# Sink attention's row sums: the step that inverts them moved ahead in VectorE's order, and their transposition behind the probabilities' in TensorE's

## The chip, the core and the metric

The kernel runs on one core of a Trainium2 chip. A core has five instruction streams that run side by side and meet only through semaphores: TensorE (PE in the profile; its weight loads have a row of their own, PEld), VectorE (DVE), ScalarE (ACT), GpSimd (POOL) and the DMA-issuing SyncE (SP). Each stream runs its instructions strictly in the order in which they were written; a waiting instruction holds back all that stand behind it. The metric is the device time of one execution in microseconds (us), the median of several runs.

## What is computed

Three layers, chained: attention with sink tokens and a sliding window over 2 batches, 8 heads, 768 positions of 64 columns; a convolutional MLP; and a mixture of four causal attention experts. The change touches the first alone:

```python
scores = scale * np.matmul(q, k.transpose(0, 1, 3, 2))
keep = is_sink | in_window            # n_sink = 4, window = 128
scores = np.where(keep, scores, -1000000000.0)
scores = scores - np.max(scores, axis=-1, keepdims=True)
a = np.exp(scores)
a = a / (np.sum(a, axis=-1, keepdims=True) + 1e-09)
return np.matmul(a, v).astype(np.float32)
...
x = _moe_ref(x=x, **moe_kwargs)       # relu(x @ w_in), 3-tap convolution, gate, @ w_out
return _moe2_ref(x=x, **moe2_kwargs)  # four experts: causal attention, top 2
```

The MLP's weights come as 64-bit floats and are converted on the chip, each into a high and a low part.

## The kernel before

**Tiles and steps.** A batch's attention goes over 6 tiles of 128 queries (qt) and, in each, over 4 pairs of heads (pr): 24 steps. A step i has stages that are spread over later steps. `a1_S` (lines 449 to 492) makes the scores: TensorE multiplies into two banks of PSUM, one for each head (L484 in the first batch, L471 in the second), VectorE adds the mask and takes the row's maximum (L486, twice), and ScalarE takes the exponential and the row's sum (L489, twice; the sums go into `su`, 8 columns for the 8 heads of a tile). `a1_T` transposes the probabilities on TensorE (L545) and copies them out of PSUM (L501, on ScalarE, tile `PT`). `a1_V` multiplies them with v (L587).

**The row sums.** They are not divided out of the probabilities; the tile's output is scaled afterwards. When the fourth pair of a tile is done, `a1_r` adds 1e-9 to the 128 x 8 sums and inverts them on VectorE (L496, L497). `a1_rT` transposes them to 8 x 128 on TensorE (L514), copies that out of PSUM (L501 on ScalarE in the first batch, L503 on VectorE in the second; tile `rT`) and sends it to memory (L518, tile `rD`). `a1_rB` reads it back, spread over 128 partitions (L525, tile `R`), and `x_norm` multiplies (L529). This happens 12 times, 6 in each batch.

**What else runs there.** In both batches' attention the MLP's weights are converted beside the steps, one weight tile of 128 x 512 after another: L339 on ScalarE, then L343, L346 and L349 on VectorE (tiles `raw` and `f64u`), then the high part on a varying engine (L507 or L509) and the low part on VectorE (L413). From the second batch's seventh step on, the MLP of the first batch runs interleaved (L753 to L797).

**What sets the order.** Nothing is scheduled at run time. `run_phases` puts each stage of each step at a time (the stage's start, plus its lag, plus the step's number times the rate), and within one time sorts by the stage's place in a list of names, the string ORD1. There `a0` is the first batch's attention, `a1` the second's, `m` the MLP; `.r`, `.rT`, `.S`, `.T` are the stages above, and `a0.misc`, `a1.misc`, `.more` and `m.misc` issue loads and the conversion's pieces. The lags are not touched: `r` runs one step after the tile's fourth pair, `rT` two steps after, in both batches.

```python
    for t in sorted(at):
        for _, _, i, fn in sorted(at[t], key=lambda c: c[:3]):
            fn(i)
...
    def a1_r(self, b, qt):
        r = self.a1s[(b, qt)]
        self.nc.vector.tensor_scalar(r, r, EPS, None, op0=ALU.add)
        self.nc.vector.reciprocal(r, r)
```

Of the kernel before, what the change touches and what calls it, by code (L numbers as in the profile page):

```python
# [74 lines left out]
LAGM = (1, 2, 3)  # L75
A2_N = 2
EVT = 'aaadadada'
ORD1 = 'm.rest a0.more a1.T a0.gather m.more m.H a1.gather a1.rB m.gate a0.xl m.Y a1.S a1.V a1.sV a1.xl a1.r a0.S a1.halo a0.sL late a0.V a0.rB a0.sV a0.xm a1.more a1.sT a0.halo a0.rT a1.xm a1.misc a1.xh a0.sT a0.T a0.misc a1.sL a0.r a1.rT m.conv m.misc a0.xh'
ORD2 = 'q1 c0.V c0.T c0.S0 c1.V c1.T c1.S0 out c0.W c0.S1 qlo c0.norm c1.W in c1.S1 q0'
ENG_G = 'pp'  # L80
WHI = 'aadaddapdpaaddda'
# [7 lines left out]
class Kernel:  # L89
# [1027 lines left out]
    def program(self, general):  # L1117
# [5 lines left out]
        with ExitStack() as ctx:  # L1123
# [89 lines left out]
            else:  # L1213
                a0, a1 = first
                src = {"a0": a0, "a1": a1, "m": m, "late": late}
                ph = self.order(ORD1, src)
            qlo = (t, t1 + 60, [(0, lambda i: self.run_qlater())], 1)
# [71 lines left out]
```

## Time and profile before

| what | value |
|---|---|
| median of 3 runs | 371.52 us (371.45 to 371.52) |
| the profiled execution: its time | 371.99 us |
| its span (first to last instruction) | 370.1 us |
| PE, DVE, ACT, POOL busy, share of the span | 97%, 74%, 71%, 32% |
| mean granted TensorE clock | 0.996 |

The first batch's attention fills the stretch from about 6 to 57 us, the second's from there to about 170 us with the MLP interleaved from 57 us on; the MLP's second half and the experts follow. The page's share for PE, 97%, counts matmuls whose ends are modelled, so it does not say by itself that TensorE is what every stage waits for. In the chain of waits TensorE's work stands almost alone from about 97 to 141 us and from about 155 us to the end; from about 57 to 95 us it is VectorE's, with turns through ScalarE; ahead of that TensorE's and VectorE's pieces alternate. What a stage waits for is read from three views: the chain of waits (which work, followed back from the end, was released last), the timeline with the idle time ahead of each instruction and who ended it, and the busy time in stretches.

### The profile page before, as it was taken

The numbers are of one execution on the slowest core, as the hardware profiler recorded it, in microseconds if no ns is written. First come the engines' busy times: TensorE is split into PE (matmuls) and PEld (weight loads), VectorE is DVE, ScalarE is ACT, GpSimd is POOL, SyncE is SP. The second block draws the span as 40 slices with busy tenths as digits, with TensorE's granted clock in tenths as the row PEclk, the third lists the DMA queues.
The fourth block names the chain that finished last, engine by engine and source line by source line (L and its number), as shares of the span: only waits on it lengthen the run. The fifth ranks groups of instructions, "written<-read, shape, count | busy, mean of one in ns | idle before, by whom it ended". The sixth has DMA issues, their size and how long they took to land.

```text
span 370.1 us, 8877 instructions
## 1 busy us (share of the span) xinstructions
PE 359.7 (97%) x3166; PEld 331.7 (90%) x3166; DVE 273.1 (74%) x850; ACT 261.2 (71%) x746; POOL 118.8 (32%) x230
## 2 busy tenths in 40 slices
PE   8999999899999999999999999999999999999994
PEld 5687877899899999999999999999999899978983
DVE  5689899999887997878756766238668688578731
ACT  4999998766886766546746766249878687849841
POOL 7014120444432342844421322500034144406310
PEclk9999999999999999999999999999999999999998
DMA  7943865353342311000211010000000010101112
GB/s 178 362 140 126 241 220 173 116 186 129 103 128 69 105 30 31 6 25 25 63 44 45 1 58 3 0 2 0 2 3 1 17 42 22 40 0 58 58 51 75
DMA packets 20404, 27.53 MB, mean 74 GB/s; under 512 B 2080, under 2 KB 12928, under 8 KB 20352
## 3 DMA queue, kind: packets, MB, share of 16 engines
q1 hardware_dynamic: 19120, 26.22, 22.2%
q10 hardware_dynamic: 1232, 0.66, 0.9%
q8 instruction: 27, 0.44, 0.5%
q14 instruction: 25, 0.20, 0.2%
HBM read 23.68 MB, written 3.19 MB: 73 GB/s over the span
## 4 chain that ended last, share of the span: by engine, by line
PE 77%; DVE 12%; ACT 5%; issue 2%; POOL 2%; DMA 1%; SPq 0%; ACTq 0%; DVEq 0%
PE psB L797 15%; PE psB L753 14%; PE psB L947 9%; PE psB L1061 5%; PE psB L1037 5%; PE psB L875 5%; PE psB L1085 4%; PE psB L587 4%; PE psB L484 4%; PE psB L545 3%; DVE P L486 3%; PE psB L1008 3%; PE psB L1007 3%; PE psB L471 2%; ACT P L489 2%
## 5 line engine op out<-in xcount | busy, mean ns | idle before, releaser
L797 PE MATMUL psB<-g,wouthf 128*128 128x256 f32 x384 | 70.5, 281 | 0.2 <-POOL g L782 0.2
L797 PEld LDWEIGHTS psB<-g,wouthf 128*128 128x128 f32 x384 | 58.9, 188 | 0.6 <-POOL g L782 0.4
L753 PE MATMUL psB<-xh,winhf 128*128 128x258 f32 x192 | 56.5, 294 | 0.0
L1025 POOL TENSOR_SCALAR P<-P,r 128x256 f32<-128x256 f32 (+5 forms) x48 | 30.3, 644 | 79.4 <-DVE r L1023 32.6
L753 PE MATMUL psB<-xh,winlf 128*128 128x258 f32 x192 | 54.3, 283 | 0.0
L753 PE MATMUL psB<-xl,winhf 128*128 128x258 f32 x192 | 54.2, 282 | 0.0
L797 PE MATMUL psB<-g,woutlf 128*128 128x256 f32 x192 | 53.8, 280 | 0.0
L489 ACT ACTIVATE P<-P,nm 128x260 f32<-128x260 f32 (+2 forms) x96 | 46.5, 486 | 10.1 <-DVE nm L486 9.9
L782 POOL TENSOR_TENSOR g<-ht,g 128x256 fp32r<-128x256 f32 x48 | 33.2, 691 | 52.4 <-ACT g L776 46.9
L1014 ACT ACTIVATE P<-P,nm 128x256 f32<-128x256 f32 (+5 forms) x48 | 32.1, 669 | 13.5 <-DVE nm L1013 7.8
L769 ACT ACTIVATE ht<-ht 128x256 f32<-128x256 f32 x48 | 20.1, 418 | 28.3 <-DVE ht L767 28.2
L774 DVE SCALAR_TENSOR_TENSOR ht<-ht 128x256 f32<-128x256 f32 x48 | 24.2, 505 | 18.8 <-ACT ht L769 18.8
L753 PEld LDWEIGHTS psB<-xh,winhf 128*128 128x128 f32 x192 | 36.4, 189 | 0.3 <-ACT ht L756 0.2
L753 PEld LDWEIGHTS psB<-xl,winhf 128*128 128x128 f32 x192 | 36.5, 190 | 0.0
L753 PEld LDWEIGHTS psB<-xh,winlf 128*128 128x128 f32 x192 | 36.2, 189 | 0.0
L797 PEld LDWEIGHTS psB<-g,woutlf 128*128 128x128 f32 x192 | 36.2, 189 | 0.0
L1010 DVE CUSTOM_DVE_ANT_0 P<-psB,causal 128x384 f32<-128x384 f32 (+3 forms) x64 | 30.3, 503 | 5.7 <-PE psB L1008 5.2
L760 POOL TENSOR_SCALAR ht<-ht,cw 128x256 f32<-128x256 f32 x24 | 15.1, 627 | 59.8 <-ACT ht L756 52.3
L767 DVE SCALAR_TENSOR_TENSOR ht<-ht,cw 128x256 f32<-128x256 f32 x48 | 28.3, 589 | 1.7
L545 PE MATMUL psB<-ident,P 128*128 128x128 f32 x176 | 29.0, 281 | 0.2
L947 PE MATMUL psB<-yh,wqh 128*128 128x256 f32 x96 | 27.2, 283 | 0.0
L947 PE MATMUL psB<-yl,wqh 128*128 128x256 f32 x96 | 27.0, 281 | 0.0
(172 smaller groups left out, 961.3 us busy)
## 6 DMA issues: line engine op xcount, KB each, us to landing
raw<-in_w_in_dram SPq DMA_DIRECT2D x8, 512.0 KB, 4.1
raw<-in_w_out_dram SPq DMA_DIRECT2D x8, 512.0 KB, 3.3
v<-in_v_dram SPq DMA_DIRECT2D x12, 256.0 KB, 4.4
R<-rD SPq DMA_DIRECT2D x24, 128.0 KB, 2.9
out_dram<-ot SPq DMA_DIRECT2D x11, 256.0 KB, 2.0
k<-in_k_dram SPq DMA_DIRECT2D x7, 260.0 KB, 3.6
raw<-in_wqkv_dram SPq DMA_DIRECT2D x8, 193.0 KB, 3.0
q<-in_q_dram SPq DMA_DIRECT2D x6, 256.0 KB, 4.5
```

What stands on the lines that cost most here:

```text
L489: nc.scalar.activation(Pt[:, j, :N], Pt[:, j, :N], AF.Exp, bias=nmx[:, j : j + 1], scale=-1.0, accum_out=sums[:, j : j + 1])
L545: nc.tensor.transpose(ps[:, j, c, :], Pt[:, j, c0 : c0 + P], self.ident)
L753: nc.tensor.matmul(ps[:, :XW], w[:, f, kc, :], x[:, kc, :], start=(i == 0), stop=(i == len(ops) - 1))
L767: nc.vector.scalar_tensor_tensor(t1, h[:, 2 : 2 + CH], self.cw[:, 2 * NF + f : 2 * NF + f + 1], t1, op0=ALU.mult, op1=ALU.add)
L769: nc.scalar.activation(t1, t1, AF.Tanh)
L774: nc.vector.scalar_tensor_tensor(t1, t1, 1.0, h[:, 1 : 1 + CH], op0=ALU.add, op1=ALU.mult)
L782: eng.tensor_tensor(g[:, 1], t1, g[:, 0].bitcast(F32), op=ALU.subtract)
L797: nc.tensor.matmul(self.m1y[d // 2][:, d % 2, :], w[:, f, d, :], g[:, k], start=(first and i == 0 and d % 2 == 0), stop=(last and i == 2), ...
L947: nc.tensor.matmul(ps, w[:, kc, c0 : c0 + P], y[:, kc, :], start=(i == 0), stop=(i == len(ops) - 1))
L1010: nc.vector.tensor_tensor_reduce(out=Pt[:, lo:hi], in0=ps[:, : hi - lo], in1=mask, scale=-1.0, scalar=BIG, op0=ALU.add, op1=ALU.min, accum ...
L1014: nc.scalar.activation(Pt[:, :N], Pt[:, :N], AF.Exp, bias=nm[:, 0:1], scale=-1.0, accum_out=sums[:, j : j + 1])
L1025: nc.gpsimd.tensor_scalar(Ps[j][:, :N], Ps[j][:, :N], r[:, j : j + 1], 1.0, op0=ALU.mult, op1=ALU.mult)
```

## The change

One string is changed, the order of the stages' names. Three names move: `a1.r` from behind `a1.xl` to ahead of `a1.S`; `a0.r` from behind `a1.sL` (that is, behind the conversion's pieces) to directly behind `a0.S`; and `a0.rT` from ahead of `a1.xm` to directly behind `a0.T`.

```diff
-ORD1 = '... m.Y a1.S a1.V a1.sV a1.xl a1.r a0.S ... a0.halo a0.rT a1.xm a1.misc a1.xh a0.sT a0.T a0.misc a1.sL a0.r a1.rT ...'
+ORD1 = '... m.Y a1.r a1.S a1.V a1.sV a1.xl a0.S a0.r ... a0.halo a1.xm a1.misc a1.xh a0.sT a0.T a0.rT a0.misc a1.sL a1.rT ...'
```

No instruction is added or taken away. On VectorE ten of the twelve pairs L496, L497 stand elsewhere (the second batch's last two stand where they stood); on TensorE five of twelve L514; on ScalarE five copies of `rT`; on SyncE one L518.

First batch, VectorE, the step after the fourth query tile's last pair (`su_470` is that tile's sums; the number behind a name is a buffer's):

```order
 L486 ISA nm_591 128x1
-L349 SCALAR_TENSOR_TENSOR f64u_500<-raw_376,f64u_500 128x512
 L496 TENSOR_SCALAR su_470<-su_470 128x8
 L497 RECIPROCAL su_470<-su_470 128x8
+L349 SCALAR_TENSOR_TENSOR f64u_502<-raw_378,f64u_502 128x512
 L486 ISA P_635,nm_636<-psB_633,m0x 128x260
```

The two small instructions stood behind the conversion's L349 and now stand ahead of it. The first batch's other five places read alike; at the first of them three conversions of 128 x 24 stand in L349's place.

First batch, TensorE, one step later, the same tile:

```order
 L484 MATMUL psB_633<-k_128,q_121 128x260
 L484 MATMUL psB_634<-k_128,q_121 128x260
-L514 MATMUL psB_643<-ident,su_470 8x128
-L545 MATMUL psB_649<-ident,P_590 128x128 x4
+L545 MATMUL psB_643<-ident,P_590 128x128 x4
+L514 MATMUL psB_650<-ident,su_470 8x128
 L484 MATMUL psB_662<-k_128,q_121 128x260
```

The transposition of the sums changed places with the four transpositions of the step's probabilities; the copies on ScalarE follow suit. So at five places; at the sixth, the batch's last tile, there is no such swap.

Second batch, VectorE, the step after the first query tile's last pair, before:

```order
L617 TENSOR_TENSOR xl_955<-R_883,xh_954 128x4x128
L486 ISA P_991,nm_992<-psB_989,m_69 128x256
L486 ISA nm_992 128x1
L486 ISA P_991,nm_992<-psB_990,m_69 128x256
L486 ISA nm_992 128x1
L496 TENSOR_SCALAR su_867<-su_867 128x8
L497 RECIPROCAL su_867<-su_867 128x8
L349 SCALAR_TENSOR_TENSOR f64u_894<-raw_762,f64u_894 128x512
```

The same place, after:

```order
L617 TENSOR_TENSOR xl_955<-R_885,xh_954 128x4x128
L496 TENSOR_SCALAR su_867<-su_867 128x8
L497 RECIPROCAL su_867<-su_867 128x8
L486 ISA P_993,nm_994<-psB_991,m_69 128x256
L486 ISA nm_994 128x1
L486 ISA P_993,nm_994<-psB_992,m_69 128x256
L486 ISA nm_994 128x1
L349 SCALAR_TENSOR_TENSOR f64u_896<-raw_764,f64u_896 128x512
```

Here the two small instructions went ahead of the step's masked scores, L486. Three more places of the second batch read alike, and TensorE's order is the same as before in this batch.

## Rows read from the trace of the kernel before

**Rows 1.** Busy time in one stretch: length, then busy us (instructions) of PE, PEld, DVE, ACT, POOL, clock, DMA:

```profile
100.00:141.00 41.00, 41.00 (x393) 38.44 (x395) 35.79 (x94) 29.41 (x87) 14.90 (x36) 1.00 0.25 79
```

**Rows 2.** Timeline of TensorE's weight loads: start, duration, engine, line, tile, [idle ahead <-releaser]:

```profile
12.69 0.08 PEld L514 LDWEIGHTS psB<-ident,su 128*8 128x8 f32 x1 [0.65 <-DVE su L497]
17.30 0.30 PEld L484 LDWEIGHTS psB<-k,q 128*128 128x128 f32 x2 [0.31 <-DMA q<-in_q_dram]
...
36.74 0.08 PEld L514 LDWEIGHTS psB<-ident,su 128*8 128x8 f32 x1 [0.64 <-ACT P L489]
...
52.75 0.08 PEld L514 LDWEIGHTS psB<-ident,su 128*8 128x8 f32 x1 [0.28 <-DVE su L497]
...
58.86 0.08 PEld L514 LDWEIGHTS psB<-ident,su 128*8 128x8 f32 x1 [0.49 <-DVE su L497]
...
71.86 0.08 PEld L514 LDWEIGHTS psB<-ident,su 128*8 128x8 f32 x1 [1.14 <-ACT P L489]
...
74.86 0.30 PEld L797 LDWEIGHTS psB<-g,wouthf 128*128 128x128 f32 x2 [0.24 <-ACT PT L501]
```

**Rows 3.** Timeline of all engines, 35 to 38 us:

```profile
35.62 0.69 DVE L349 SCALAR_TENSOR_TENSOR f64u<-raw,f64u 128x512 int32<-128x512 int32 x1
35.90 0.50 ACT L489 ACTIVATE P<-P,nm 128x260 f32<-128x260 f32 x1
36.23 0.16 DVE L496 TENSOR_SCALAR su<-su 128x8 f32<-128x8 f32 x1
36.42 0.20 DVE L497 RECIPROCAL su<-su 128x8 f32<-128x8 f32 x1
36.87 0.42 PEld L545 LDWEIGHTS psB<-ident,P 128*128 128x128 f32 x4
37.26 0.74 PEld L484 LDWEIGHTS psB<-k,q 128*128 128x128 f32 x4
```

**Rows 4.** Timeline of all engines, 44 to 45 us:

```profile
44.49 0.59 ACT L501 COPY PT<-psB 128x512 f32<-128x512 f32 x1 [0.35 <-PE psB L545]
44.98 0.43 DVE L486 CUSTOM_DVE_ANT_0 P<-psB,m1x 128x260 f32<-128x260 f32 x1 [0.72 <-PE psB L484]
```

**Rows 5.** Timeline of DVE and POOL, 26 to 30 us, and at 51.7 us:

```profile
26.37 0.69 DVE L349 SCALAR_TENSOR_TENSOR f64u<-raw,f64u 128x512 int32<-128x512 int32 x1
27.16 1.27 POOL L295 TENSOR_TENSOR vsr<-vs,vsr 32x512 fp32r<-32x512 f32 x1 [2.73 <-issue]
29.09 1.28 POOL L295 TENSOR_TENSOR vsr<-vs,vsr 32x512 fp32r<-32x512 f32 x1
29.18 1.46 DVE L343 TENSOR_SCALAR f64u<-f64u 128x512 int32<-128x512 int32 x1 [0.49 <-ACT f64u L339]
...
51.70 0.69 DVE L349 SCALAR_TENSOR_TENSOR f64u<-raw,f64u 128x512 int32<-128x512 int32 x1
51.75 0.68 POOL L626 CAST xl<-xl 128x4 fp32r<-128x4 f32 x1
```

**Rows 6.** Timeline of DVE and ACT, 57 to 60 us:

```profile
57.20 0.19 ACT L489 ACTIVATION_READ_ACCUMULATOR P<-P,nm 128x1 f32 x1
57.71 0.42 DVE L486 CUSTOM_DVE_ANT_0 P<-psB,m 128x256 f32<-128x256 f32 x1
58.17 0.51 ACT L489 ACTIVATE P<-P,nm 128x256 f32<-128x256 f32 x1 [0.53 <-DVE nm L486]
58.40 0.17 DVE L496 TENSOR_SCALAR su<-su 128x8 f32<-128x8 f32 x1
58.72 0.64 DVE L349 SCALAR_TENSOR_TENSOR f64u<-raw,f64u 128x512 int32<-128x512 int32 x1
59.96 0.43 DVE L343 TENSOR_SCALAR f64u<-f64u 128x512 int32<-128x512 int32 x1 [0.60 <-ACT f64u L339]
```

**Rows 7.** Timeline of ACT, 73 and 92 us:

```profile
73.27 0.42 ACT L769 ACTIVATE ht<-ht 128x256 f32<-128x256 f32 x1 [1.07 <-DVE ht L767]
...
92.35 1.07 ACT L810 COPY y<-psB 128x512 f32<-128x512 f32 x2
```

More of the change, by code (lines that the diff above doesn't have):

```diff
@@ L77 @@
 EVT = 'aaadadada'
-ORD1 = 'm.rest a0.more a1.T a0.gather m.more m.H a1.gather a1.rB m.gate a0.xl m.Y a1.S a1.V a1.sV a1.xl a1.r a0.S a1.halo a0.sL late a0.V a0.rB a0.sV a0.xm a1.more a1.sT a0.halo a0.rT a1.xm a1.misc a1.xh a0.sT a0.T a0.misc a1.sL a0.r a1.rT m.conv m.misc a0.xh'
+ORD1 = 'm.rest a0.more a1.T a0.gather m.more m.H a1.gather a1.rB m.gate a0.xl m.Y a1.r a1.S a1.V a1.sV a1.xl a0.S a0.r a1.halo a0.sL late a0.V a0.rB a0.sV a0.xm a1.more a1.sT a0.halo a1.xm a1.misc a1.xh a0.sT a0.T a0.rT a0.misc a1.sL a1.rT m.conv m.misc a0.xh'
 ORD2 = 'q1 c0.V c0.T c0.S0 c1.V c1.T c1.S0 out c0.W c0.S1 qlo c0.norm c1.W in c1.S1 q0'
```

## The prediction, on record before the changed kernel ran

> **What bounds the kernel now.** I read the chain of waits first. From about 97 to 141 us and from 155 us to the end it runs on TensorE almost alone; in the stretch from 100 to 141 us TensorE is busy 41.00 of 41.00 us [rows 1]. There, an instruction of VectorE that comes 0.3 us sooner or later moves nothing. The change can only tell where TensorE really waits, or where another engine sets the pace: in the first batch's attention, up to 57 us, where TensorE, ScalarE and VectorE are all nearly full, and from 57 to 95 us, where the chain runs on VectorE with turns through ScalarE.
>
> The second view is the idle time ahead of each weight load, for the twelve L514. Seven have none to speak of (a gap of 0.17 us stands ahead of most groups). Five waited: 0.65, 0.64, 0.28, 0.49 and 1.14 us [rows 2], 3.20 us in all. This is the most that the change can give back directly. The question for each is whether that wait is what the next stage needed.
>
> **What each part costs or gives.** Nothing is added, so every term is a shift. The price of a moved pair L496, L497 is the time from the start of L496 to the start of what follows it: 58.72 - 58.40 = 0.32 us [rows 6]; at 36.2 us it reads the same way, 0.16 and 0.20 us long with their overlap [rows 3].
>
> First batch, the wait of 0.64 us at 36.74. L514 stood ahead of the probabilities' transpositions and waited for L497, which stood behind L349; those transpositions started at 36.87, the next scores' weights at 37.26 [rows 3]. In the new order the transpositions wait for their exponentials alone: the second one begins at 35.90 and takes 0.50 us, so they end at about 36.40 [rows 3], and TensorE starts some 0.1 us later, at 36.5. Then come L514 (0.08 to 0.13 us) and the scores, at about 37.05 in place of 37.26. The gain is about 0.2 us. It is not eaten up on the way: at 44.49 ScalarE waited 0.35 us for TensorE and at 44.98 VectorE waited 0.72 us for it [rows 4], so both follow a TensorE that is earlier by up to 0.35 us, and from there VectorE runs without a gap into the second batch.
>
> First batch, the wait of 0.65 us at 12.69. The transpositions' own exponentials end only about 0.1 us before, so little is won, and at 17.30 TensorE waits 0.31 us for a load of q [rows 2], which no part of the change issues sooner. Term: 0. The wait of 0.28 us at 52.75: TensorE gets L514 earlier, but the scores behind it go to VectorE, whose L349 and scores need the same sum of time in either order. Term: 0. The other three places of this batch had no wait. Term: 0. The copy of `rT` now stands behind that of `PT`, so `rD` leaves about half a microsecond later; the first one is queued behind loads anyway, and SyncE's order otherwise changes at one place only. I put this at 0: between the issue of `R` and its use several microseconds of steps lie.
>
> First batch, third place, at 26.37. There was no wait of TensorE here, but a neighbour. L349 moves back by 0.32 us and then ends at 26.37 + 0.32 + 0.69 = 27.38, less an overlap of up to 0.08, that is 27.30 to 27.38. GpSimd's L295 wants to start at 27.16 [rows 5]. The row at 51.75 shows what happens then: a cast of 4 columns by GpSimd, begun 0.05 us after an L349, took 0.68 us and ended with it (52.43 against 52.39). So L295 would lose 0.14 to 0.22 us, and with it the chain behind it on GpSimd, up to the second L295 at 29.09, which would start at 29.23 to 29.31. In the trace that second L295 started 0.09 us before VectorE's L343 (29.18), and L343 took 1.46 us [rows 5] where the same instruction takes 0.43 us [rows 6]. L343 would now come first, by 0.05 to 0.13 us, and end about 1.0 us sooner. What is then late next is TensorE, which runs without a wait from there to the 0.64 us at 36.74: scores, masks and exponentials follow it, and of the 1.0 us there remains what makes the exponentials at 35.90 earlier, about 0.3 us. The transpositions then start behind the scores at about 36.3, the next scores at 36.8 in place of 37.26: the gain of this batch becomes 0.48 us in place of 0.2 us.
>
> The Trainium skill, "SBUF — State Buffer", section "Who interferes with whom", says that an instruction of VectorE with two inputs in SBUF and one of GpSimd that reads SBUF exclude each other, and that whichever is issued first keeps the ports for its whole length. It names this case's pairs (L349 with L295, and L343 as a two-port instruction), and the 0.68 and 1.46 us agree with it. By that rule alone the swap at 29.18 is certain, and the first batch gives 0.48 us.
>
> By the rows the swap hangs on 0.05 to 0.13 us between two engines that are not in step, and I give it 60%.
>
> Second batch, first place, at 57.71. Here the chain of waits goes through what the change delays. VectorE masks the scores (57.71), ScalarE, idle for 0.53 us, starts the exponentials at 58.17, then converts (L339), and VectorE, idle for 0.60 us, goes on with L343 at 59.96 [rows 6]. The pair now stands ahead of the masks, so masks, exponentials, L339 and L343 all come 0.32 us later. The sums that the pair needs are read out at 57.39 [rows 6], so no wait comes on top. The 0.49 us that TensorE no longer waits at 58.86 [rows 2] buys nothing, since L343 does not depend on it. Term: +0.32 us, and VectorE carries it to about 95 us, where TensorE waits for it in turn.
>
> Second batch, second place, the wait of 1.14 us at 71.86. L514 would come about 0.8 us earlier (the pair no longer behind both masks). But at 74.86 TensorE waits 0.24 us for ScalarE's copy [rows 2], which stands behind L769, which waited 1.07 us for VectorE [rows 7]; VectorE's sum up to there is the same in either order. The 0.8 us turn into a longer wait at 74.86. Term: 0. The delayed exponentials end inside the 1.07 us. Third place, at 92: the exponentials stand behind two copies that last to 92.35 + 1.07 = 93.42 [rows 7], the masks end before that even with 0.32 us more. Term: 0. Fourth place, at 109 us: TensorE sets the pace [rows 1]. Term: 0.
>
> **Sum.** With the swap at 29.18: -0.48 + 0.32 = -0.16 us; without it: -0.2 + 0.32 = +0.12 us. The profiled execution took 371.99 us with a span of 370.1 us; the terms are differences and go over to the median of the runs, 371.52 us: 371.36 or 371.64 us. I take the likelier one, rounded to 371.4 us: no change that can be measured, since about 0.2% (0.74 us) is what a measurement of this kernel can tell from none.
>
> **The rivals.** First, faster: TensorE and not VectorE sets the pace from 72 us on. For it speaks that TensorE has idle time of 1.14 and 0.24 us only between 71 and 75 us; against it the order in which the chain of waits passes there, on VectorE throughout. Then the 0.8 us at 71.86 stay won: -0.48 + 0.32 - 0.8 = -0.96 us, 370.6 us. Chance 16%.
>
> Second, slower: the delayed masks are on the path at all four places of the second batch, not at one. Its price is 0.32 us each, its point the one at which the next instruction of VectorE waits for the exponentials rather than for the copies ahead of them. Then 4 x 0.32 = 1.28, less 0.2 to 0.48: +0.8 to +1.08 us, 372.3 to 372.6 us. Against it stand the 1.07 us of slack and the copies up to 93.42 [rows 7]. Chance 12%.
>
> Third, the lock rule's other outcome: L343 still comes second. That is the 371.64 us above, inside the forecast. Fourth, the change doesn't do what it says, because L514 then waits somewhere else: its operands are ready by 36.1 at the fourth place, so I see no such wait; the time would be that of before plus 0.32, 371.8 us, inside the forecast as well.
>
> **Chances and range.** Within 0.2%: 72%; faster by more: 16%; slower by more: 12%. The range takes in the first rival and the low end of the second: 370.6 to 372.3 us.
>
> **What the profile after would show.** Right: no idle time ahead of L514 at 36.7; an L343 of about 0.4 us near 29.2; the masks of the second batch's first step about 0.3 us later against the end of L617 ahead of them; a longer wait of TensorE near 74.9. Wrong: TensorE's stretch from 97 us on starting earlier by 0.7 us or more (the first rival), or ScalarE waiting for masks at 71, 92 and 109 us (the second). The forecast falls if a collision of VectorE and GpSimd that the trace does not show now appears or goes elsewhere, at about 1 us each.

## The result, and the profile after

The changed kernel took 373.69 us, median of 6 runs (373.39 to 374.58), beside 371.63 us for the kernel before, also of 6: a ratio of 1.0056, 95% interval 1.0040 to 1.0071. Run again beside other kernels it came out at 1.0047 (1.0029 to 1.0064). It is slower by about 1.9 us. The prediction, 371.4 us and "no change", was wrong, and the time lies outside its range.

The profiled execution took 373.5 us with a span of 371.7 us, against 371.99 and 370.1 us before. PE, DVE, ACT and POOL are busy 97%, 73%, 70% and 32%, against 97%, 74%, 71% and 32%: no engine has more instructions, so the time went into waits. The chain of waits shows where to look first. Its pieces in the changed kernel (start, us, what; dots for pieces left out):

```profile
38.76 0.46 ACT PT L501
...
39.75 2.68 DMA v<-in_v_dram
42.48 0.88 PE psB L587 x12
...
53.93 4.11 DMA vs<-in_vs_dram
...
58.92 0.68 ACT P L489 x3
59.60 0.67 ACT f64u L339 x2
...
60.31 5.62 DMA raw<-in_w_out_dram
...
66.00 0.54 issue
...
66.76 0.43 DVE f64u L343
```

In the kernel before, the same stretch has one piece of DMA, 0.47 us of `rD`; here three loads stand in the chain. The page's chain of waits gives DMA 6% of the span, 1% before; about half of the 6% are two loads of q in the first 17 us. What the three have in common is SyncE. Its issues in the kernel before (start, duration, line):

```profile
38.79 0.30 SPq L518 DMA_DIRECT2D rD<-rT  x1
39.14 0.81 SPq L280 DMA_DIRECT2D v<-in_v_dram  x2
...
54.60 0.29 SPq L518 DMA_DIRECT2D rD<-rT  x1
54.95 0.65 SPq L255 DMA_DIRECT2D k<-in_k_dram  x1
...
56.85 1.25 SPq L525 DMA_DIRECT2D R<-rD  x2
59.39 0.33 SPq L372 DMA_DIRECT2D raw<-in_w_out_dram  x1
```

and in the changed one:

```profile
39.41 0.30 SPq L518 DMA_DIRECT2D rD<-rT  x1
39.75 0.81 SPq L280 DMA_DIRECT2D v<-in_v_dram  x2
...
53.53 0.33 SPq L255 DMA_DIRECT2D k<-in_k_dram  x1
53.93 0.41 SPq L284 DMA_DIRECT2D vs<-in_vs_dram  x1
54.63 0.29 SPq L518 DMA_DIRECT2D rD<-rT  x1
...
58.95 1.26 SPq L525 DMA_DIRECT2D R<-rD  x2
60.31 0.55 SPq L372 DMA_DIRECT2D raw<-in_w_out_dram  x1
```

The copy of `rT` now stands behind that of `PT`, so L518 leaves 0.62 us later at 39 us, and v, queued behind it, is issued 0.61 us later. At the batch boundary L518 went behind k and vs, 516 KB together. It leaves at the same time, but `R`, which needs its 4 KB to have landed, can be issued 4.3 us behind it in place of 2.25 us, and `raw`, which stands behind `R`, 0.92 us later.

The places that answer to [rows 2, 3] and [rows 6], TensorE's weight loads, then VectorE and ScalarE. First two rows of the kernel before:

```profile
42.25 0.85 PEld L587 LDWEIGHTS psB<-PT,v 128*64 128x64 f32 x16 [0.34 <-ACT P L489]
...
64.75 0.66 ACT L339 ACTIVATE f64u<-raw 128x512 f32<-128x512 f32 x1
```

The changed kernel:

```profile
36.28 0.60 PEld L545 LDWEIGHTS psB<-ident,P 128*128 128x128 f32 x4
36.85 0.09 PEld L514 LDWEIGHTS psB<-ident,su 128*8 128x8 f32 x1
36.96 0.74 PEld L484 LDWEIGHTS psB<-k,q 128*128 128x128 f32 x4
...
42.48 0.64 PEld L587 LDWEIGHTS psB<-PT,v 128*64 128x64 f32 x12 [0.33 <-DMA v<-in_v_dram]
```

```profile
57.61 0.16 DVE L496 TENSOR_SCALAR su<-su 128x8 f32<-128x8 f32 x1
57.80 0.20 DVE L497 RECIPROCAL su<-su 128x8 f32<-128x8 f32 x1
58.04 0.42 DVE L486 CUSTOM_DVE_ANT_0 P<-psB,m 128x256 f32<-128x256 f32 x1
58.51 0.51 ACT L489 ACTIVATE P<-P,nm 128x256 f32<-128x256 f32 x1 [0.84 <-DVE nm L486]
...
60.29 0.43 DVE L343 TENSOR_SCALAR f64u<-f64u 128x512 int32<-128x512 int32 x1 [0.87 <-ACT f64u L339]
...
65.95 0.69 ACT L339 ACTIVATE f64u<-raw 128x512 f32<-128x512 f32 x1 [0.77 <-DMA raw<-in_w_out_dram]
...
66.76 0.43 DVE L343 TENSOR_SCALAR f64u<-f64u 128x512 int32<-128x512 int32 x1 [1.74 <-ACT f64u L339]
```

The wait of 0.64 us ahead of L514 is gone and the scores behind it come 0.30 us earlier (36.96 against 37.26). Some five microseconds on, L587 waits 0.33 us for v. At 57.6 us the pair stands ahead of the masks, and L343 comes 0.33 us later (60.29 against 59.96), as forecast. Then `raw` is late, and L339 waits 0.77 us for it.

### The profile page after: what moved, and what is told of

Its sections match the earlier page's. It is cut to its first block, busy times and chain, and to the rows that moved or that the text cites. A ratio compares the mean times of both kernels' runs of the same rounds, so it can differ in the third digit from the quotient of the medians.

```text
span 371.7 us, 8871 instructions
## 1 busy us (share of the span) xinstructions
PE 360.8 (97%) x3166; PEld 332.1 (89%) x3166; DVE 272.1 (73%) x850; ACT 261.3 (70%) x746; POOL 118.5 (32%) x230
## 4 chain that ended last, share of the span: by engine, by line
PE 70%; DVE 11%; ACT 7%; DMA 6%; issue 2%; POOL 2%; ACTq 0%; SPq 0%; DVEq 0%
PE psB L797 15%; PE psB L753 14%; PE psB L947 9%; PE psB L1061 5%; PE psB L1037 5%; PE psB L875 5%; PE psB L1085 4%; ACT P L489 3%; DMA q<-in_q_dram 3%; PE psB L587 2%; PE psB L1008 2%; PE psB L1007 2%; PE psB L545 2%; DVE P L486 2%; PE psB L471 2%
## 5 line engine op out<-in xcount | busy, mean ns | idle before, releaser
L753 PE MATMUL psB<-xh,winlf 128*128 128x258 f32 x192 | 54.3, 283 | 0.0
L774 DVE SCALAR_TENSOR_TENSOR ht<-ht 128x256 f32<-128x256 f32 x48 | 24.2, 504 | 18.9 <-ACT ht L769 18.9
L753 PEld LDWEIGHTS psB<-xl,winhf 128*128 128x128 f32 x192 | 36.5, 190 | 0.0
L1010 DVE CUSTOM_DVE_ANT_0 P<-psB,causal 128x384 f32<-128x384 f32 (+3 forms) x64 | 30.2, 502 | 6.1 <-PE psB L1008 5.6
L545 PE MATMUL psB<-ident,P 128*128 128x128 f32 x176 | 30.0, 283 | 1.5 <-ACT P L489 1.3
L767 DVE SCALAR_TENSOR_TENSOR ht<-ht,cw 128x256 f32<-128x256 f32 x48 | 27.5, 573 | 1.7
```

Of the source, the lines that this page charges most:

```text
L545: nc.tensor.transpose(ps[:, j, c, :], Pt[:, j, c0 : c0 + P], self.ident)
L753: nc.tensor.matmul(ps[:, :XW], w[:, f, kc, :], x[:, kc, :], start=(i == 0), stop=(i == len(ops) - 1))
L767: nc.vector.scalar_tensor_tensor(t1, h[:, 2 : 2 + CH], self.cw[:, 2 * NF + f : 2 * NF + f + 1], t1, op0=ALU.mult, op1=ALU.add)
L774: nc.vector.scalar_tensor_tensor(t1, t1, 1.0, h[:, 1 : 1 + CH], op0=ALU.add, op1=ALU.mult)
L1010: nc.vector.tensor_tensor_reduce(out=Pt[:, lo:hi], in0=ps[:, : hi - lo], in1=mask, scale=-1.0, scalar=BIG, op0=ALU.add, op1=ALU.min, accum ...
```

## The experiments

The first four kernels tested two theories. Theory 1: SyncE's order at the batch boundary costs the time (rD behind k and vs, so R and raw late). Theory 2: the delayed masks and the collisions of VectorE and GpSimd cost it. Each kernel is the one before with parts of the change alone, all in the string ORD1. 0.001 of a ratio is 0.37 us.

**SyncE's place alone**: L518 goes behind k and vs, no instruction of a computing engine moves.

```diff
-... a0.halo a0.rT a1.xm a1.misc a1.xh ...
+... a0.halo a1.xm a1.misc a0.rT a1.xh ...
```

> Before, with a0.rT moved behind a1.misc and nothing else: the one instruction that changes its place is SyncE's L518 at 54.6 us, which now stands behind the loads of k and vs. Theory 1 (the small write of the sums' inverses is queued behind 768 KB of loads, the read-back L525 that waits for it holds up SyncE, and the weight load behind it comes about 1 us late, so that ScalarE's L339 waits for it near 65 us): +1.0 to +1.8 us on a span of 370.1 us, with a wait of 0.5 to 1 us of L339 for raw. Theory 2 (the delayed masks of the second batch and the collisions of VectorE and GpSimd that they shift): within 0.2 us of before, no such wait.

Measured: 372.28 us, 1.0004 (0.9990 to 1.0018). In its trace raw was issued at 60.52 us, as late as in the changed kernel, and yet L339 did not wait for it: it started at 65.63 us, when raw had landed. Alone, the late order costs nothing that can be measured (the interval allows up to 0.7 us); theory 1 in its simple form falls. (Its expectation counts 768 KB of loads ahead of L518; k and vs are 516 KB, q stands behind it.)

**The second batch's part alone.**

```diff
-... m.Y a1.S a1.V a1.sV a1.xl a1.r a0.S ...
+... m.Y a1.r a1.S a1.V a1.sV a1.xl a0.S ...
```

> Before, with a1.r alone moved ahead of a1.S (only VectorE's order changes, at four places of the second batch). Theory 1: +0.3 us, within 0.2% of before. Theory 2: +1.3 to +2 us.

Measured: 372.9 us, 1.0016 (1.0006 to 1.0026). Between 20 and 349 us its trace loses some 0.3 us at 57.7 us and 0.28 us at 92 us, and nothing else: 0.6 us together, which is what the ratio says. (This execution, the slowest of its twelve, lost another 0.5 us ahead of 20 us and 0.6 us behind 349 us, where nothing moved.)

**The first batch's part alone**, SyncE's place with it.

```diff
-... a0.S a1.halo ... a0.halo a0.rT a1.xm ... a0.T a0.misc a1.sL a0.r a1.rT ...
+... a0.S a0.r a1.halo ... a0.halo a1.xm ... a0.T a0.rT a0.misc a1.sL a1.rT ...
```

> The first batch's two moves without a1.r. Theory 1: +1.0 to +1.8 us, since SyncE's L518 stands behind the loads as in the changed kernel. Theory 2: within 0.2 us of before, a little below it.

Measured: 372.8 us, 1.0012 (1.0002 to 1.0023): a part that by the prediction was to gain 0.2 to 0.48 us loses. L587 waits 0.68 us for v at 42.86 us.

**The whole change with SyncE's old order at the boundary** (against the changed kernel, `a1.misc` moved behind `a0.rT` as well; on ScalarE this also lets one L339 change places with a copy of `PT`).

```diff
-... a1.xm a1.misc a1.xh a0.sT a0.T a0.rT a0.misc ...
+... a1.xm a1.xh a0.sT a0.T a0.rT a1.misc a0.misc ...
```

> The changed kernel with a1.misc moved behind a0.rT: VectorE's and TensorE's order are those of the changed kernel, SyncE's is that of before (on ScalarE one L339 changes places with one PT copy). Theory 1: +0.2 to +0.5 us against before, that is the masks' 0.32 us alone; no wait of L339 for raw near 65 us. Theory 2: the loss stays, +1.6 to +2.1 us.

Measured: 373.07 us, 1.0025 (1.0012 to 1.0037), under half of the change's loss. So the boundary's order seems to matter after all, but together with the rest. From here on theory 3 was: what matters is what is queued behind L518 on SyncE, at every place where it comes later.

**The changed kernel again, and the first batch taken apart.** The next four shared their runs of before (372.06 us).

> The changed kernel once more, beside the next three, for a ratio against the same runs of the kernel before and a second profile. Theory 3 (what stands behind L518 on SyncE): the copy of rT behind that of PT sends rD 0.6 us later, and the loads queued behind it come late at two places: v (L280, about 39.7 us, landing at 42.4 to 42.9 for L587, 0.3 to 0.7 us of wait there) and, through L525, raw (L372, about 60.3 us, which ScalarE's L339 at 65 to 66 us needs). Then this profile shows both waits again, L339 idle 0.2 to 0.8 us ahead of 65.9 us, and the ratio is 1.004 to 1.007. Rival (a straggler): the late raw was an accident of one execution, in which one of 16 DMA engines finished 1.4 us behind the others; then L339 does not wait here, and the ratio stays at 1.004 to 1.007 for another reason.

Measured: 1.0047. L587 waited 0.74 us for v, but L339 did not wait for raw: there the rival was right, the 0.77 us belonged to one execution. (In it the last of raw's 16 parts landed at 65.93 us, 1.43 us behind the fifteenth; here raw landed at 64.57 us, though it was issued later.)

The pair ahead of L349 in the first batch, and nothing else; L514, `rT` and SyncE stay:

```diff
-... a0.S a1.halo ... a1.sL a0.r a1.rT ...
+... a0.S a0.r a1.halo ... a1.sL a1.rT ...
```

> The kernel before with the pair L496, L497 ahead of L349 in the first batch alone; rT, rD and SyncE's order stay. Theory 3: L514 no longer waits at 36.7 us, nothing on SyncE is later (L518 there at 38.4 to 38.8 us, v landed by 41.8 us, no wait of L587 for v), so the gain of 0.2 to 0.5 us arrives: ratio 0.9986 to 0.9996. Rival (VectorE's sum decides, TensorE's wait is worth nothing): 1.000 within 0.0005, with the masks at 44.98 us where they were.

Measured: 371.57 us, 0.9988 (0.9976 to 1.0001). The first batch's part with SyncE's old order at the boundary:

```diff
-... a0.S a1.halo ... a0.halo a0.rT a1.xm a1.misc a1.xh a0.sT a0.T a0.misc a1.sL a0.r a1.rT ...
+... a0.S a0.r a1.halo ... a0.halo a1.xm a1.xh a0.sT a0.T a0.rT a1.misc a0.misc a1.sL a1.rT ...
```

> The first batch's part of the change (pair ahead of L349, L514 and the copy of rT behind the probabilities'), with SyncE's order at the batch boundary as before. Theory 3: v still stands behind the later L518, L587 waits 0.3 to 0.7 us for v at 42.5 us, and the gain at 36.7 us is eaten: ratio 1.000 to 1.001, masks at 44.98 us not earlier than before; against the run of the first batch's part with the boundary's order changed (1.0012) it is lower by what that order costs, 0.0005 to 0.001. Rival (the first batch's part loses its time elsewhere, in collisions): the same ratio as that run, 1.0012.

Measured: 372.04 us, 0.9998 (0.9987 to 1.0009): 0.0014 under the same part with the boundary's new order. The two ran beside different runs of before and their intervals overlap, so that the boundary's order costs this part anything is suggested and not shown. In this one execution v was in time, against theory 3, and L529 waited 0.69 us for R.

The same with one load of v a step earlier, ahead of L518:

```diff
-(7, 'q', 0, 3), (17, 'v', 0, 4), (11, 'q', 0, 4),
+(7, 'q', 0, 3), (16, 'v', 0, 4), (11, 'q', 0, 4),
```

> The same as the run with the first batch's part and the old boundary order, with one load moved: v of the fifth query tile is issued one step earlier, ahead of L518. Theory 3: L587 no longer waits for v at 42.5 us, the masks at 44.98 us come 0.2 to 0.4 us earlier than in the kernel before, ratio 0.9988 to 0.9998, that is 0.001 under the run without the moved load. Rival: the two runs have the same ratio, since the load only moves another one (q, raw) back.

Measured: 372.04 us, 1.0003 (0.9993 to 1.0013). In the trace the wait is gone and the masks at 44.98 us come 0.48 us earlier than before, as theory 3 said; the median did not follow. The rival was right on the time, but not for its reason: up to 320 us the trace keeps that gain (0.53 us from 20 us on), and then loses 0.35 us ahead of L1010, at a gap that is described below.

**Two ways to undo the boundary.** Theory 4 adds theory 3's late loads to the 0.59 us of the second batch's part. These shared the runs of before, 372.42 us.

> The whole change but with SyncE's old order at the batch boundary, once more, so that it stands beside the next run against the same runs of before. Theory 4 (three parts: a1.r ahead of the scores costs 0.31 us at 57.7 us and 0.28 us at 92 to 94 us; v late for L587 eats the first batch's gain of about 0.2 us; and the later R and raw at the batch boundary, with next to no slack left, cost 0.8 to 1.1 us on top in the mean of the executions): the boundary's part is gone, ratio 1.0015 to 1.003. Rival (no such part; the spread of the executions made it up): 1.0045 to 1.0055, as the changed kernel.

Measured: 1.0022 (1.0011 to 1.0033). And the changed kernel with one load, vs, a step later, so that L518 stands behind k alone:

```diff
-            if i == 1:
+            if i == 2:
                 self.load_vs(1, self.qkv[1])
```

> The changed kernel with one load moved: vs of the second batch is issued one step later, so that L518 at the batch boundary stands behind one load of 260 KB on SyncE instead of two of 516 KB together. Theory 4: R is issued 0.5 to 1.0 us sooner (57.9 to 58.5 us in place of 58.9 to 59.3), raw stands no longer behind it (59.7 to 59.9 us in place of 60.3 to 60.7), and the ratio falls to that of the kernel with SyncE's old order, 1.0015 to 1.003. Rival: it stays at 1.0045 to 1.0055.

Measured: 372.98 us, 1.0018 (1.0005 to 1.0031). SyncE in that run:

```profile
53.72 0.33 SPq L255 DMA_DIRECT2D k<-in_k_dram  x1
54.81 0.29 SPq L518 DMA_DIRECT2D rD<-rT  x1
55.16 0.34 SPq L284 DMA_DIRECT2D vs<-in_vs_dram  x1
...
58.32 1.25 SPq L525 DMA_DIRECT2D R<-rD  x2
59.95 0.33 SPq L372 DMA_DIRECT2D raw<-in_w_out_dram  x1
```

Both ways of bringing R and raw forward take the ratio from 1.0047 to 1.0056 down to about 1.002: 0.8 to 1.4 us. The changed kernel did not run beside these; by the medians themselves the difference is 0.5 to 1.0 us.

> The kernel before with the pair ahead of L349 in the first batch alone, once more, to see whether its gain of 0.0012 (interval up to 1.0001) holds. Theory 4: 0.9983 to 0.9996. Rival (no gain, TensorE's shorter waits are worth nothing): 0.9995 to 1.0005.

Measured: 371.67 us, 0.9982 (0.9974 to 0.9991). With the earlier v on top:

> The same with v of the fifth query tile issued one step earlier, since L587 still waited 0.18 us for it at 42.3 us. Theory 4: no wait for v there, masks at 44.98 us another 0.1 to 0.3 us earlier, ratio 0.0003 to 0.0008 under the run beside it. Rival: no difference, as the moved load had given none in the earlier pair of runs (1.0003 against 0.9998).

Measured: 371.77 us, 0.9981 (0.9972 to 0.9989): no difference. In the trace v was in time, and R came later (issued at 50.73 us, 48.48 in the kernel before), so that L529 waited 0.59 us for it. That the moved load moved the wait there is not shown: the pair alone has R at 50.16 us in one trace and at 48.66 us in the other.

**The pair alone, moved ahead of L349 in the first batch, beats both kernels**, by 0.4 to 0.7 us against before in two sessions (the first interval just reaches 1). Its TensorE and SyncE:

```profile
36.12 0.08 PEld L514 LDWEIGHTS psB<-ident,su 128*8 128x8 f32 x1
36.33 0.47 PEld L545 LDWEIGHTS psB<-ident,P 128*128 128x128 f32 x4
36.76 0.74 PEld L484 LDWEIGHTS psB<-k,q 128*128 128x128 f32 x4
...
38.76 0.30 SPq L518 DMA_DIRECT2D rD<-rT  x1
39.11 0.80 SPq L280 DMA_DIRECT2D v<-in_v_dram  x2
```

L514 does not wait any more, though it still stands ahead of the transpositions, and L518 leaves when it did in the kernel before. The half of the change that undid this was to move L514. That it did so through the later copy of `rT`, and not through TensorE's order, rests on one trace: with L514 moved and v ahead of it (the experiment above), the kernel gains 0.53 us from 20 to 320 us, the pair alone 0.30 and 0.52 us in its two.

**Three more traces of the changed kernel, one of the kernel before.**

> A third look at the changed kernel, at where the part of its time goes that after_vs takes away. Theory 4: the loads behind L518 at the batch boundary show in the trace as one of three waits, L529 for R at 64 us, L339 for raw at 66 us, or L343 to L346 colliding with GpSimd's L295 in another place behind such a wait, together 0.3 to 1.0 us between 57 and 74 us; at least two of these three looks have one. Rival: the stretch from 57.7 to 74 us gains nothing against before but the 0.31 us of the masks, in all three.

> A fourth look. Theory 4: as for the third, 0.3 to 1.0 us between 57 and 74 us on top of the masks' 0.31 us. Rival: nothing on top of it.

> A fifth look. Theory 4: as for the third, 0.3 to 1.0 us between 57 and 74 us on top of the masks' 0.31 us. Rival: nothing on top of it.

> A second look at the kernel before. Theory 4: no wait for R at 64 us and none for raw at 65 us (slack of about 1.2 us), L587 without a wait for v at 42.3 us, L776 at 92 us idle 0.75 us ahead, no 0.34 us ahead of L1010 at 326.6 us. Rival: such waits come and go in the kernel before as well, so that they are no mark of the change.

The table follows single instructions of VectorE through five traces of the changed kernel: the time there less the time in the first trace of before, in us. (L343 at 60.29 against 59.96 is the 0.33 of the first.)

| instruction, its time before | before, 2nd | 1st | 2nd | 3rd | 4th | 5th |
|---|---|---|---|---|---|---|
| L486, 20.10 | 0.06 | 0.12 | 0.28 | 0.25 | -0.21 | 0.25 |
| L486, 44.98 | 0.14 | 0.02 | 0.60 | 0.51 | 0.14 | -0.06 |
| L529, 54.32 | 0.18 | 0.02 | 0.60 | 0.90 | 0.61 | -0.06 |
| L343, 59.96 | 0.17 | 0.33 | 0.91 | 1.22 | 0.92 | 0.26 |
| L774, 69.64 | 0.17 | 0.90 | 0.92 | 1.23 | 1.50 | 0.26 |
| L774, 91.53 | 0.15 | 1.07 | 0.88 | 1.20 | 1.46 | 0.22 |
| L774, 95.27 | 0.15 | 1.35 | 1.17 | 1.48 | 1.74 | 0.50 |
| L486, 119.20 | 0.15 | 1.31 | 1.13 | 1.45 | 1.71 | 0.47 |
| L1010, 326.55 | 0.07 | 1.66 | 1.49 | 1.81 | 2.08 | 0.82 |
| L1010, 348.92 | 0.08 | 1.66 | 1.48 | 2.22 | 2.47 | 1.24 |

From 20 us on the five lose 1.68 us on average, near what the medians say; the kernels with the boundary undone lose 1.14 to 1.19 us in their three traces. The differences from line to line are the parts, as means of the five:

- 20 to 45 us: +0.10, where the pair alone gains 0.28 and 0.43 us in its two traces. L587 waits 0.33, 0.74, 0.68 and 0.76 us for v in four of the five, never in the two traces of before.
- 45 to 54 us: +0.17. L529 waits for R in the third and fourth trace. R is issued behind the rD of 47 us, which is 0.4 to 1.1 us later in the five; in the kernel before R had landed 0.12 us ahead of its use. But how long rD takes there varies by itself: R is issued 1.6 us behind it in the kernel before, and 3.6 us behind it in the first experiment (SyncE's place alone), where the order up to there is that of before and L529 waits 0.24 us for R as well. So this part is not shown to be the change's.
- 54 to 60 us: +0.31, in each trace 0.31 or 0.32: the delayed masks.
- 60 to 70 us: +0.23, from two traces: the late raw in the first, and in the fourth TensorE's clock (below). Theory 4 had wanted 0.3 to 1.0 us from late loads there in two of the last three traces. One showed, 0.28 us ahead of L529 for R in the fifth, and it cost nothing by 69.64 us; so this is not borne out.
- 92 to 95 us: +0.28, in every trace.
- 119 to 326 us: +0.36, in every trace, at one instruction.
- 340 us: +0.24, from three traces with some 0.4 us; it comes and goes in other kernels too.

The wait for R in the fourth trace:

```profile
54.92 0.69 DVE L529 TENSOR_TENSOR R<-psB,R 128x512 f32<-128x512 f32 x1 [0.39 <-DMA R<-rD]
```

The two constant losses, L776 on ScalarE and L1010 on VectorE, in the kernel before:

```profile
92.04 0.41 ACT L776 CAST g<-ht 128x256 fp32r<-128x256 f32 x1 [0.75 <-DVE ht L774]
...
326.55 0.56 DVE L1010 CUSTOM_DVE_ANT_0 P<-psB,causal 128x384 f32<-128x384 f32 x1
```

and in the changed one:

```profile
93.39 0.41 ACT L776 CAST g<-ht 128x256 fp32r<-128x256 f32 x1 [1.03 <-DVE su L496]
...
328.21 0.56 DVE L1010 CUSTOM_DVE_ANT_0 P<-psB,causal 128x384 f32<-128x384 f32 x1 [0.34 <-PE psB L1008]
```

and L1010 in the kernel with the first batch's part and the earlier v, whose second batch is unchanged:

```profile
326.29 0.56 DVE L1010 CUSTOM_DVE_ANT_0 P<-psB,causal 128x384 f32<-128x384 f32 x1 [0.34 <-PE psB L1008]
```

The releasers named there mislead. The idle time of 1.03 us ahead of L776 came also in the kernel with the pair of the first batch and the earlier v, whose second batch is unchanged too; there the trace names L486. Kernels traced twice or more behaved alike each time (the changed one five times, its version with the old boundary twice, the pair alone and the kernel before twice each without either gap). So, as far as these traces go, the gaps belong to a built program and not to an execution, and they are not what the moved instruction waits for. What sets them stays open.

## Why the prediction was wrong

**The step that failed** is the one on SyncE: "The copy of `rT` now stands behind that of `PT`, so `rD` leaves about half a microsecond later ... I put this at 0: between the issue of `R` and its use several microseconds of steps lie." The half microsecond was right (0.62 us at 39 us); the price was not. I asked only for R's own slack, by the number of steps. I did not name what is queued behind L518 on its engine: v at 39 us, and, through the waiting L525, raw at 59 us. Nor did I read when R landed against its use, 0.12 us ahead of it at 54.3 us. "SyncE's order otherwise changes at one place only" was true and was taken for harmless; at that place 4 KB went behind 516 KB, and R was issued 2.1 us later. Undoing that place alone brings 0.8 to 1.4 us by the ratios. No rival held it. By the five traces the step is worth about 0.6 us of the miss: 0.30 us at 20 to 45 us (0.10 lost in place of 0.2 gained), 0.17 us at 45 to 54 us, which may not all be its own, and 0.11 us in the mean for the late raw. Another 0.12 us in the mean is TensorE's clock. The other 0.88 us, the two gaps and the stretch at 340 us, stand in no term of the sum, and their cause stays open.

**The first batch's gain** was right where it was named: 0.30 us at 37 us, against 0.2 forecast, and 0.28 and 0.43 us at 45 us with the pair alone. With L514 moved too, v's wait eats it in four traces of five. The move of L514 was costed as part of the gain; it is not needed for it.

**The swap at 29.18**, given 60%, came in one trace of the five. First the usual case, then the fifth trace:

```profile
29.23 1.27 POOL L295 TENSOR_TENSOR vsr<-vs,vsr 32x512 fp32r<-32x512 f32 x1
29.29 1.49 DVE L343 TENSOR_SCALAR f64u<-f64u 128x512 int32<-128x512 int32 x1 [0.47 <-ACT f64u L339]
```

```profile
29.73 0.43 DVE L343 TENSOR_SCALAR f64u<-f64u 128x512 int32<-128x512 int32 x1 [0.79 <-ACT f64u L339]
29.75 1.54 POOL L295 TENSOR_TENSOR vsr<-vs,vsr 32x512 fp32r<-32x512 f32 x1
```

Where it came, L343 took 0.43 us as forecast. It started 0.44 us later than in the first trace (29.73 against 29.29) and the transpositions at 36.5 us only 0.26 us later (36.54 against 36.28), so some 0.2 us of the 1.0 us won remained, near the 0.3 forecast. What failed is its trigger. The first L295, at 27.27, was to lose 0.14 to 0.22 us to an L349 that now overlaps it; it lost 0.04 us (1.31 us in place of 1.27), though they overlapped for 0.18 us. The forecast took the whole overlap as lost. In every such overlap at 27 and 29 us, in all traces, the second instruction loses some 0.15 us less than the overlap, and [rows 5] showed it: L295 ends at 30.37, 1.19 us behind the start of L343, which lost 1.03 us. By that 0.14 to 0.22 us of overlap cost 0.07 us at most, the second L295 starts at 29.16 at the latest, and L343 at 29.18 still comes second. In the fifth trace L349 itself came later, the overlap was 0.27 us and L295 lost 0.13 us; so it was in the trace of the first batch's part with the old boundary, where the swap came too. The Trainium skill, "SBUF — State Buffer", section "Who interferes with whom", lets whichever is issued first keep the ports for its whole length; the pair at 29 us agrees with it in both orders, and at 27.3 us the second instruction is held up as well, but for some 0.15 us less than the overlap of the two rows.

**The second batch's first place**: +0.32 us forecast, 0.31 or 0.32 us in each of five traces; the mechanism and the size were right. The other three places were put at 0, and VectorE neither gains nor loses at 72 us (69.64 to 91.53: -0.03 or -0.04 us in four traces, +0.17 us in the first). The longer wait of TensorE near 74.9 us did not come: in the first trace L514 still waits 0.82 us at 72.19, the transpositions behind it wait 0.93 and 0.29 us for the exponentials, and none is left at 74.9. At 92 us 0.28 us appear in every kernel with `a1.r` moved, at L776; as the same gap came once without that move, it is not put down to the masks.

**The rivals.** TensorE's pace from 72 us (faster) did not show. The delayed masks at all four places came nearest in time (372.3 to 372.6 us), for a reason that the traces don't bear out: the masks cost at one place.

**The range** was too narrow because the one term with an unread slack was entered as 0 without two ends. Bounded by the nearest row, v landing 0.6 us later than its 41.82 us for a use at 42.25, it would have been 0.2 us for that place alone, and more wherever the load itself takes longer.

**What stays open**: the two gaps of 0.28 and 0.34 us, and most of the boundary. Undoing it brings 0.8 to 1.4 us by the ratios, while of five traces one has a late raw (0.77 us of waiting, 0.57 us lost by 70 us) and the other four none. In the timed runs a mean clock of 0.995 or less stands beside 4 of 17 executions of the changed kernel and 7 of 104 of the kernel before. The four are among the slower ones: without them the second session's median is 373.06 us in place of 373.94. Whether the later loads bring the fall about was not tried.

## What to carry to other kernels

When an instruction moves on a computing engine, follow its result to the queue that sends it, and list what is issued behind it there: every load behind a waiting send inherits its delay, and its slack is to be read as landing time against use, not counted in steps. Take a change apart before judging it: here one of its three moves gains, and the other two cost more than it gives. Take several traces before a wait of half a microsecond is called the cause, and search them for gaps that sit far from every moved instruction: two of them were over a third of this loss.

## What the runs showed of the hardware

TensorE's clock fell once in mid-kernel, in the fourth trace of the changed kernel (length, PE busy and instructions, granted clock, DMA):

```profile
55.00:60.00 5.00, 3.79 (x34) 1.00 0.63 219
60.00:62.00 2.00, 1.97 (x10) 0.51 0.59 152
62.00:64.00 2.00, 2.00 (x16) 0.64 0.68 250
64.00:69.00 5.00, 5.00 (x54) 1.00 0.44 134
```

From 60 to about 63.5 us it ran at the lower of its levels, 1.2 GHz, and the kernel lost 0.58 us in that stretch that no wait accounts for. Ahead of it TensorE had been busy 3.79 of 5 us. In the kernel before it was 4.34 us and in the third trace of the changed one 3.92 us, and in both the clock stayed at 2.4 GHz.

A write of 4 KB that is issued behind 516 KB of loads held up the read that needs it for 4.1 to 4.3 us from its issue in the five traces of the changed kernel, against 2.25 and 2.4 us ahead of the same loads in the two of before. The order is not all: ahead of the loads it took 3.6 and 4.0 us in the traces of two other kernels (the pair with the earlier v, the first batch's part with the old boundary).

Where L349 or L343 on VectorE and L295 on GpSimd overlapped, the one that started second took longer by the overlap less 0.13 to 0.16 us, in both orders.

Two idle times of 0.28 and 0.34 us, ahead of L776 and L1010, came and went with the program built, the same in each of its traces, without an instruction there that waited for anything new.
